# Soft-MoE after a gated recurrence: two weights moved behind the stream, and filler matmuls in TensorE's waits

## The chip, the cores and the metric

The kernel runs on one core of a Trainium2 chip. The core has five engines with queues of their own: TensorE (PE; its weight loads are shown apart as PEld), VectorE (DVE), ScalarE (ACT), GpSimd (POOL) and SyncE (SP). They share an on-chip memory (SBUF), TensorE writes into an accumulation memory (PSUM), and 16 DMA engines move data between HBM and SBUF. The metric is the device time of one execution in microseconds; lower is better. The version before takes 200.91 us (median of 13 runs, 199.79 to 202.6).

## The reference

Two layers, one after the other. The first is an elementwise gated recurrence over time for 4 sequences of 5056 tokens with 256 channels:

```
sig = 1/(1+exp(-f_logit));  f = lb + (1-lb)*sig;  i = 1 - f
for t: h = f[:,t]*h + i[:,t]*x[:,t];  y[:,t] = h
```

The second is a soft mixture of experts on the 4 x 5056 = 20224 rows of y: 8 experts with 4 slots each, 32 slots in all.

```
logits = y @ phi                        # [20224, 32]
d = softmax of logits over all rows;    slot_input = d.T @ y      # [32, 256]
slot_out[e] = relu(slot_input[e] @ w1[e]) @ w2[e]                 # w1: 256x1024, w2: 1024x256
c = softmax of logits over the slots;   out = c @ slot_out        # [20224, 256]
```

x and f_logit are 20.7 MB each, the eight pairs of expert weights 16.8 MB in f32, and the output 20.7 MB. All must be read or written once. No output row can be made before the experts are done, and they need the slot inputs, which need every row of y.

## The kernel before

**The stream.** Time is cut into 10 groups of 512 tokens (the ninth, `odd`, has 448), and each group has 4 units, one for each sequence: 40 units, numbered n = group * 4 + sequence. Inputs come in pairs of units, into three pair buffers of x and three of f (`ld`, bufs=3); SyncE issues them with `load(n + 6)` at every even n. A unit goes through these steps:

- `gate` (L199, ScalarE): s = sigmoid(-f), for two units at once from unit 6 on; an activation-table load stands around each change between sigmoid and exp.
- `enter` (L210, GpSimd): u = s * x.
- `s_to_channels`, `u_to_channels` (L225, TensorE): four 128x128 transposes each, so that channels lie on partitions; s for two units at every even n, u for one unit at every n.
- `decay` (L248, ScalarE): the factor a from s. `scan` (L258, VectorE): the recurrence, two instructions of 512 steps.
- `to_tokens` (L271, TensorE): four transposes of h back, into the single PSUM buffer `hp`; `keep_tokens` (L285) copies them into `ht`, on VectorE for even sequences and on ScalarE for odd ones. The next `to_tokens` needs that buffer empty.
- per group: `logits` (L299), `exps` (L308, into `etall`), `weights_to_tokens` (L320, L323) and `slots` (L349, which adds up 32 slots x 256 channels in PSUM, `slot_ps`).

The order of all this is written out by hand: the loop over n names, for each engine, what it does in that unit, and each engine runs its instructions in that order (the pools allow no reordering: `manual_schedule`). So in an even unit n TensorE does `to_tokens(n - 1)`, eight transposes of s for units n + 2 and n + 3, and four of u for unit n + 1, on which the next scan waits. An odd unit has no transposes of s. The units before and after a group's logits and slots have little TensorE work; the change calls for filler in some of them.

**The expert weights.** They are 16 transfers (w1 of experts 1 to 8, then w2 of experts 1 to 8), issued by GpSimd with a cast from f32 to bf16, each 1.05 MB read and 0.52 MB written. `W_AT` says in which unit how many are issued; the issue stands in GpSimd's queue after `enter(n + 3)`.

**The experts.** After the last unit, TensorE turns the slot sums into `sin`, and then: hidden layer of all experts (L551), transposes (L566), second layer of experts 1 to 4 packed into one pass (L587), then of experts 5 to 8 one after the other (L597, index j = 0 to 3, eight matmuls each). After j = 1 come the remaining row sums of the softmax over slots (L332, `row_sums`) into the PSUM tile `tail`. `spin` and `idle` are matmuls whose result nobody reads.

**The output.** `slot_out` (L610) is the last result that everything waits for; then TensorE multiplies (L630, L679), VectorE and ScalarE scale (L620, L624, L684, L690), and SyncE issues the stores.

The constant `rep` (four 32 x 128 copies of an identity, L87) is first used after the stream, at L522.

Of the kernel before, what the change touches and what calls it, by code (L numbers as in the profile page):

```python
# [10 lines left out]
BF16 = mybir.dt.bfloat16  # L11
# [7 lines left out]
def kernel(  # L19
# [10 lines left out]
    nc = tc.nc  # L30
    B, S, D = x.shape
    E = moe_w1.shape[0]
    F = moe_w1.shape[2]
    NS = moe_phi.shape[1]
    SPE = NS // E
    P = 128
# [5 lines left out]
    n_unit = n_grp * B  # L42
# [25 lines left out]
    ident_f = consts.tile([P, P], F32, name="ident_f")  # L68
# [12 lines left out]

    nc.vector.tensor_copy(ident, ident_f)

    def rep_constants():
        for b in range(B):
            blk = ident_f[ds(b * NS, NS), ds(b * NS, NS)]
            nc.vector.tensor_copy(rep[ds(b * NS, NS)],  # L87
                                  blk.unsqueeze(1).broadcast_to([NS, B, NS]))

    ones = consts.tile([P, B], BF16, name="ones")  # L90
    nc.vector.memset(ones, 0.0)
# [47 lines left out]
            nc.tensor.matmul(dst[:, ds(0, w)], w1_sb[0][:, 0, :P], w1_sb[0][:, 0, :w],  # L139
                             start=True, stop=True, skip_group_check=True)  # L140

    W_AT = {9: 1, 15: 1, 21: 1, 27: 1, 31: 1, 33: 1, 34: 3, 35: 1, 36: 6}
    w_next = [0]
    ctx.enter_context(tc.manual_schedule())

# [3 lines left out]
    with tc.tile_pool(name="sp2", bufs=3) as sp2, \  # L149
# [9 lines left out]
        slot_bank = pslot.tile([P, 2, D], F32, name="slot_ps")  # L159
        slot_ps = slot_bank[:, 0]  # L160

        def idle(k):
            for _ in range(k):
                nc.tensor.matmul(slot_bank[:, 1], w1_sb[0][:, 0, :P], w1_sb[0][:, 0, :D],
                                 start=False, stop=False, skip_group_check=True)
        xs, fs, sts, uts, pss, psus, hs, hps, hts, lgs, ets = ({} for _ in range(11))

        def tokens(src, n, k):
# [94 lines left out]
        SINGLE = 6  # L263
# [17 lines left out]
        def keep_tokens(n):  # L281
            g, b = divmod(n, B)
            n_p = rows(g)
            copy = nc.scalar.copy if b % 2 and n >= SINGLE - 2 else nc.vector.tensor_copy
            copy(hts[g][:n_p, b].rearrange("p r d -> p (r d)").bitcast(F32),  # L285
                 hps.pop(n)[:n_p].rearrange("p r c -> p (r c)"))

# [67 lines left out]
        def unit(f, m):  # L355
            if 0 <= m < n_unit:
                f(m)
# [63 lines left out]
        for n in range(n_unit):  # L421
            if n < SINGLE - 2:
                if n:
                    unit(to_tokens, n - 1)
                    unit(u_to_channels, n + 1)
                s_to_channels(n + 2)
                gate(n + 3, 1 if n + 3 < SINGLE else 2)
                decay(n + 2, 1)
                if n % 2 == 0:
                    unit(load, n + AHEAD)  # L430
                unit(enter, n + 3)
            else:
                end = n >= n_unit - 6
                if n % 2 == 0:
                    unit(load, n + AHEAD)
                    if n == SINGLE - 2:
                        to_tokens(n - 1)
                        keep_tokens(n - 1)
                    if not end:
                        unit(gate, n + 4)  # L440
                else:
                    unit(decay, n + 1)
                    if n == n_unit - 5:
                        gate(n + 3)
                        exps(odd - 1)
                if not end and n != n_unit - 7:
                    group(exps, n - 2)

                unit(enter, n + 3)
                for _ in range(W_AT.get(n, 0)):  # L450
                    load_w(w_next[0])
                    w_next[0] += 1

                if n == n_unit - 2:
                    unit(u_to_channels, n + 1)
                if n != SINGLE - 2:
                    unit(to_tokens, n - 1)
                if n == n_unit - 2:
                    keep_tokens(n - 1)
                if n % 2 == 0:  # L460
                    unit(s_to_channels, n + 2)
                    unit(s_to_channels, n + 3)
                if n != n_unit - 2:
                    unit(u_to_channels, n + 1)
                if n in (n_unit - 5, n_unit - 4):
                    idle(4)
                if n == n_unit - 2:
                    tail = psp.tile([P, 2, G], F32, name="tail", tag="sp")
                    rs_ps = tail[:, 0, ds(0, n_grp * R * B)].rearrange(
                        "p (q b) -> p q b", b=B)  # L470
                    late_ps, odd_ps = (
                        tail[:, 1].bitcast(BF16)[:, ds(i * R * P, R * P)].rearrange(
                            "p (r s) -> p r s", r=R) for i in range(2))
                    logits(odd)
                    exps(odd)
                    slots(odd - 1)
                    spin(tail[:, 1], 1, G)
                    odd_weights()
                elif not end:
                    group(logits, n - 1)  # L480
# [4 lines left out]
                late_weights([0, 1, 2], nc.scalar.copy)  # L485

            unit(scan, n)
            if n == 0:
                rep_constants()
            if n not in (SINGLE - 2, n_unit - 2):  # L490
                unit(keep_tokens, n - 1)
            if n == n_unit - 3:
# [32 lines left out]
    with tc.tile_pool(name="ew", bufs=1) as ew, \  # L525
# [69 lines left out]
        for j in range(Q):  # L595
# [8 lines left out]
            if j == 1:  # L604
                for i in range(1, len(blocks)):
                    row_sums(i)
                q = n_grp * R - 1
                nc.vector.reciprocal(rrow[:, wide_r:q], rs_ps[:, wide_r:q])
                nc.vector.reciprocal(rrow[:, q, ds(0, B // 2)], rs_ps[:, q, ds(0, B // 2)])
        nc.vector.tensor_scalar_mul(slot_out, so_ps, rcs)  # L610
# [141 lines left out]
```

## Time and profile before

| what | value |
|---|---|
| time, median of 13 runs | 200.91 us (199.79 to 202.6) |
| time of the profiled execution | 200.91 us |
| its span, first to last instruction | 199.1 us |
| TensorE busy / its weight loads | 133.5 us / 95.9 us |
| VectorE busy | 146.0 us |
| ScalarE busy | 137.8 us |
| GpSimd busy | 100.7 us |
| HBM read, written | 58.23 MB, 20.71 MB |
| mean granted TensorE clock | 0.839 |

The stream takes the first 130 us, the experts follow to 145.3, the output goes on to the end. A row by slices has 40 digits of 5 us each, in tenths of the slice; PEclk is the TensorE clock granted by the throttle, in tenths of full speed. A row by windows has the stretch and its length, then busy time and count of each engine (PE, PEld, DVE, ACT, POOL), the granted clock, the share of the DMA engines that was busy (it reads slightly over 1 when they are full) and the GB/s written. A timeline row has start, length, engine, line, operation, tiles and shapes, count, and in brackets how long the engine stood idle before it and what ended that. The chain of waits is followed back from the last instruction; its rows have start, length and what. L numbers are lines of the kernel before.

### The profile page before, as it was taken

What the parts mean: (1) busy time and instruction counts of PE and PEld (TensorE: products, weight loads), DVE (VectorE), ACT (ScalarE), POOL (GpSimd) and SP (SyncE); (2) the same over time, 40 slices, a digit from 0 to 9 for tenths busy, and PEclk for the clock granted to TensorE, in tenths of its full rate; (3) what the DMA queues carried; (4) which work ended last, traced back from release to release, by engine and by line L of the source; (5) the groups of instructions that cost most, each with busy time, mean ns of one, the idle gap of its engine ahead of it and who ended that gap; (6) DMA issues with size and microseconds to landing.
All of it is one profiled execution on the core that took longest, in us unless ns stands there. A gap on an engine that the chain in (4) does not pass through costs nothing.

```text
span 199.1 us, 3008 instructions
## 1 busy us (share of the span) xinstructions
PE 133.5 (67%) x1073; PEld 95.9 (48%) x1073; DVE 146.0 (73%) x168; ACT 137.8 (69%) x194; POOL 100.7 (51%) x72
## 2 busy tenths in 40 slices
PE   0585463975869667585976876999979999960000
PEld 0364352853657556464766555676853533410000
DVE  1699899699997999979999899915267877850000
ACT  2688666999988999599996498444057889990000
POOL 2388586894989379962995849950030000000000
PEclk9999999699996999979998899999995555555555
DMA  4999999999999999999999999999639999999995
GB/s 181 414 420 420 421 420 417 420 417 311 416 417 376 358 419 416 317 413 411 408 312 406 322 231 214 206 216 214 129 112 384 435 444 421 421 421 457 434 421 214
DMA packets 17614, 70.74 MB, mean 355 GB/s; under 512 B 2096, under 2 KB 3120, under 8 KB 16704
## 3 DMA queue, kind: packets, MB, share of 16 engines
q1 hardware_dynamic: 15120, 62.13, 76.2%
q0 software_dynamic: 2336, 8.42, 21.1%
q8 instruction: 8, 0.13, 0.2%
q14 instruction: 6, 0.05, 0.1%
q10 hardware_dynamic: 144, 0.00, 0.0%
HBM read 58.23 MB, written 20.71 MB: 396 GB/s over the span
## 4 chain that ended last, share of the span: by engine, by line
PE 35%; DVE 28%; DMA 15%; issue 8%; ACT 4%; SPq 1%; ACTq 0%; DVEq 0%
DVE h L258 21%; PE op L679 12%; DMA f_t<-in_f_logit_dram 10%; PE hp L271 4%; DMA x_t<-in_x_dram 4%; DVE ht L285 4%; PE sp L225 4%; PE op L630 2%; PE up L225 2%; PE so_ps L597 2%; ACT oc L690 1%; PE tail L332 1%; SPq L189 1%; PE hi_ps L551 1%; DVE et L323 1%
## 5 line engine op out<-in xcount | busy, mean ns | idle before, releaser
L210 POOL TENSOR_TENSOR u_t<-s_t,x_t 128x1024 bf16<-128x1024 bf16 (+1 forms) x39 | 82.4, 2128 | 28.2 <-ACT s_t L199 19.9
L258 DVE TENSOR_TENSOR_SCAN h<-a,h,up 128x512 bf16<-128x512 f32 (+1 forms) x72 | 86.3, 1250 | 5.4 <-PE up L225 3.8
L271 PE MATMUL hp<-ident_f,h 128*128 128x128 f32 (+1 forms) x160 | 30.8, 318 | 31.3 <-DVE ht L285 19.3
L199 ACT ACTIVATE s_t<-f_t 128x2048 bf16<-128x2048 f32 (+2 forms) x23 | 38.4, 1672 | 15.1 <-DMA f_t<-in_f_logit_dram 12.9
L248 ACT ACTIVATE a<-sp,nomlb 128x1024 f32<-128x1024 bf16 (+2 forms) x46 | 43.3, 994 | 3.0 <-PE sp L225 1.6
L271 PEld LDWEIGHTS hp<-ident_f,h 128*128 128x128 f32 (+1 forms) x160 | 22.9, 208 | 41.3 <-DVE ht L285 23.8
L225 PE MATMUL sp<-ident_f,s_t 128*128 128x128 f32 x144 | 23.7, 313 | 9.4 <-ACT s_t L199 6.1
L679 PE MATMUL op<-slot_bd,etall 64*128 64x512 bf16 x62 | 24.9, 622 | 0.3 <-ACT oc L690 0.2
L225 PEld LDWEIGHTS sp<-ident_f,s_t 128*128 128x128 f32 x144 | 19.8, 164 | 10.8 <-issue 6.0
L225 PE MATMUL up<-ident_f,u_t 128*128 128x128 f32 x144 | 24.3, 295 | 0.7 <-POOL u_t L210 0.7
L690 ACT ACTIVATE oc<-op,rrow 128x256 f32<-128x256 f32 x60 | 22.7, 488 | 2.1 <-PE op L679 1.5
L684 DVE TENSOR_TENSOR oc<-op,rrow 128x1024 f32<-128x1024 f32 x16 | 19.3, 1222 | 5.3 <-PE op L679 5.3
L225 PEld LDWEIGHTS up<-ident_f,u_t 128*128 128x128 f32 x144 | 18.9, 155 | 1.8 <-POOL u_t L210 1.1
L285 DVE COPY ht<-hp 128x512 f32<-128x512 f32 (+1 forms) x22 | 14.7, 669 | 2.1 <-PE hp L271 2.1
L679 PEld LDWEIGHTS <-etall 64*128 64x128 bf16 x62 | 9.1, 155 | 14.7 <-issue 12.6
L285 ACT COPY ht<-hp 128x512 f32<-128x512 f32 (+1 forms) x18 | 10.3, 575 | 4.7 <-PE hp L271 4.6
L624 ACT ACTIVATE ob<-op,rrow 128x256 f32<-128x256 f32 x16 | 6.3, 479 | 7.9 <-PE op L630 7.8
L258 DVE TENSOR_TENSOR_SCAN h<-a,up 128x512 bf16<-128x512 f32 x8 | 9.4, 1210 | 0.7 <-PE up L225 0.7
L612 POOL TENSOR_SCALAR slot_bd<-slot_out,parity 128x256 bf16<-128x256 bf16 x2 | 1.8, 920 | 13.4 <-DVE slot_out L610 13.4
L299 PE MATMUL lg<-h,phi 128*32 128x512 bf16 (+1 forms) x80 | 7.3, 414 | 0.0
L630 PE MATMUL op<-slot_out,etall 32*128 32x256 bf16 x32 | 5.9, 339 | 1.0 <-DVE slot_out L610 0.6
L349 PE MATMUL slot_ps<-ht,et 128*32 128x256 bf16 (+1 forms) x144 | 5.5, 274 | 0.8 <-DVE et L323 0.8
(98 smaller groups left out, 118.2 us busy)
## 6 DMA issues: line engine op xcount, KB each, us to landing
f_t<-in_f_logit_dram SPq DMA_DIRECT2D x36, 512.0 KB, 10.2
x_t<-in_x_dram SPq DMA_DIRECT2D x36, 512.0 KB, 10.5
out_dram<-oc SPq DMA_DIRECT2D x6, 2048.0 KB, 12.7
w_sb<-in_moe_w_dram POOLq DMA_DIRECT2D x16, 512.0 KB, 8.2
out_dram<-oc SPq DMA_DIRECT2D x4, 896.0 KB, 5.2
out_dram<-ob SPq DMA_DIRECT2D x1, 2048.0 KB, 8.3
f_t<-in_f_logit_dram SPq DMA_DIRECT2D x4, 384.0 KB, 7.7
x_t<-in_x_dram SPq DMA_DIRECT2D x4, 384.0 KB, 7.1
```

The costliest lines, as they stand in the source:

```text
L199: nc.scalar.activation(s_t, f_t, ACT.Sigmoid, scale=-1.0)
L210: nc.gpsimd.tensor_tensor(uts[n][:, :r], s_t[:, :r], x_t[:, :r], ALU.mult)
L225: nc.tensor.transpose(ps[:, :, r], t[:, r], ident_f)
L248: nc.scalar.activation(decays[n // 2, o][:, ds(n % 2, k), :T], sp[:, ds(n % 2, k), :T, o], ACT.Identity, scale=nomlb[:, ds(o, 1)], bias=1.0)
L258: nc.vector.tensor_tensor_scan(h[:, :T, o], decays[n // 2, o][:, n % 2, :T], up[:, :T, o], hs[n - B][:, ds(used(n // B - 1) - 1, 1), o] if ...
L271: nc.tensor.transpose(hp[:n_p, r], hw[:, :n_p, r], ident_f)
L285: copy(hts[g][:n_p, b].rearrange("p r d -> p (r d)").bitcast(F32), hps.pop(n)[:n_p].rearrange("p r c -> p (r c)"))
L299: nc.tensor.matmul(lg[ds(b * NS, NS), :], phi[:, o], hs[g * B + b][:, :T, o], start=o == 0, stop=o == DC - 1, skip_group_check=True)
L630: nc.tensor.matmul(op[:, j], ew[:, :, r + j], slot_out[ds(b * NS, NS)], start=True, stop=True, skip_group_check=True)
L679: nc.tensor.matmul(op[:, i_r].rearrange("p u d -> p (u d)"), ew[:, :, r + i_r], slot_bd[ds(j * 2 * NS, 2 * NS)].rearrange("s u d -> s (u d)"),
L684: nc.vector.tensor_tensor(ob[:, :, ds(r, k)].rearrange("p u r d -> p r u d"), op[:, ds(0, k)], scale[:, ds(r, k)].unsqueeze(3).broadcast_t ...
L690: nc.scalar.activation(ob[:, u, r + i_r], op[:, i_r, u], ACT.Copy, scale=scale[:, r + i_r, ds(u, 1)])
```

## The change

- `W_AT`: of the weights issued before unit 30, those at 9, 15, 21 and 27 become two, at 17 and 25. Six are issued at units 30 to 34 (before: five at units 31 to 34), none at 35, and eight instead of six at 36.
- Fillers: after the transposes of u, units 5 to 35 with n mod 8 in 1, 2, 5, 6, 7 (20 units) get five 256-column matmuls each. The operands of `idle` are now the identity and `rep` instead of the first weight, so that it waits for no weight.
- `rep` is therefore built at the start, by GpSimd, a quarter in each of units 0 to 3 behind `enter(n + 3)`, instead of by VectorE in unit 0.
- 28 matmuls of 32 columns (`SPINS`) go behind the row sums, between the second layers of experts six and seven (j = 1 and j = 2).
- `keep_tokens` changes engine for six units: 9, 17, 25 go from ScalarE to VectorE, and 12, 20, 28 from VectorE to ScalarE.
- In unit 3, ScalarE does `decay(5)` before the first paired gate instead of after it.

```diff
--- before.py
+++ after.py
@@ -81,11 +81,9 @@
 
     nc.vector.tensor_copy(ident, ident_f)
 
-    def rep_constants():
-        for b in range(B):
-            blk = ident_f[ds(b * NS, NS), ds(b * NS, NS)]
-            nc.vector.tensor_copy(rep[ds(b * NS, NS)],
-                                  blk.unsqueeze(1).broadcast_to([NS, B, NS]))
+    def rep_constants(b):
+        blk = ident_f[ds(b * NS, NS), ds(b * NS, NS)]
+        nc.gpsimd.tensor_copy(rep[ds(b * NS, NS)], blk.unsqueeze(1).broadcast_to([NS, B, NS]))
 
     ones = consts.tile([P, B], BF16, name="ones")
     nc.vector.memset(ones, 0.0)
@@ -139,7 +137,8 @@
             nc.tensor.matmul(dst[:, ds(0, w)], w1_sb[0][:, 0, :P], w1_sb[0][:, 0, :w],
                              start=True, stop=True, skip_group_check=True)
 
-    W_AT = {9: 1, 15: 1, 21: 1, 27: 1, 31: 1, 33: 1, 34: 3, 35: 1, 36: 6}
+    SPINS = 28
+    W_AT = {17: 1, 25: 1, 30: 1, 31: 1, 32: 1, 33: 2, 34: 1, 36: 8}
     w_next = [0]
     ctx.enter_context(tc.manual_schedule())
 
@@ -159,10 +158,12 @@
         slot_bank = pslot.tile([P, 2, D], F32, name="slot_ps")
         slot_ps = slot_bank[:, 0]
 
-        def idle(k):
-            for _ in range(k):
-                nc.tensor.matmul(slot_bank[:, 1], w1_sb[0][:, 0, :P], w1_sb[0][:, 0, :D],
-                                 start=False, stop=False, skip_group_check=True)
+        rep_bf = rep.rearrange("p b s -> p (b s)").bitcast(BF16)
+
+        def idle(k, first=False):
+            for i in range(k):
+                nc.tensor.matmul(slot_bank[:, 1], ident, rep_bf,
+                                 start=first and i == 0, stop=False, skip_group_check=True)
         xs, fs, sts, uts, pss, psus, hs, hps, hts, lgs, ets = ({} for _ in range(11))
 
         def tokens(src, n, k):
@@ -281,7 +282,10 @@
         def keep_tokens(n):
             g, b = divmod(n, B)
             n_p = rows(g)
-            copy = nc.scalar.copy if b % 2 and n >= SINGLE - 2 else nc.vector.tensor_copy
+            by_scalar = b % 2 and n >= SINGLE - 2
+            if 2 * B < n < n_unit - 2 * B and n % (2 * B) in (1, B):
+                by_scalar = not by_scalar
+            copy = nc.scalar.copy if by_scalar else nc.vector.tensor_copy
             copy(hts[g][:n_p, b].rearrange("p r d -> p (r d)").bitcast(F32),
                  hps.pop(n)[:n_p].rearrange("p r c -> p (r c)"))
 
@@ -424,11 +428,15 @@
                     unit(to_tokens, n - 1)
                     unit(u_to_channels, n + 1)
                 s_to_channels(n + 2)
-                gate(n + 3, 1 if n + 3 < SINGLE else 2)
+                if n + 3 < SINGLE:
+                    gate(n + 3, 1)
                 decay(n + 2, 1)
+                if n + 3 == SINGLE:
+                    gate(n + 3)
                 if n % 2 == 0:
                     unit(load, n + AHEAD)
                 unit(enter, n + 3)
+                rep_constants(n)
             else:
                 end = n >= n_unit - 6
                 if n % 2 == 0:
@@ -464,6 +472,8 @@
                     unit(u_to_channels, n + 1)
                 if n in (n_unit - 5, n_unit - 4):
                     idle(4)
+                elif SINGLE - 2 < n < n_unit - 4 and n % (2 * B) in (1, 2, 5, 6, 7):
+                    idle(5, n == SINGLE - 1)
                 if n == n_unit - 2:
                     tail = psp.tile([P, 2, G], F32, name="tail", tag="sp")
                     rs_ps = tail[:, 0, ds(0, n_grp * R * B)].rearrange(
@@ -485,8 +495,6 @@
                 late_weights([0, 1, 2], nc.scalar.copy)
 
             unit(scan, n)
-            if n == 0:
-                rep_constants()
             if n not in (SINGLE - 2, n_unit - 2):
                 unit(keep_tokens, n - 1)
             if n == n_unit - 3:
@@ -605,6 +613,7 @@
                 for i in range(1, len(blocks)):
                     row_sums(i)
                 q = n_grp * R - 1
+                spin(tail[:, 1], SPINS, NS)
                 nc.vector.reciprocal(rrow[:, wide_r:q], rs_ps[:, wide_r:q])
                 nc.vector.reciprocal(rrow[:, q, ds(0, B // 2)], rs_ps[:, q, ds(0, B // 2)])
         nc.vector.tensor_scalar_mul(slot_out, so_ps, rcs)
```

## The prediction

> **What bounds the kernel now.** I read first the page's rows by slices of the span, for what is never idle.
>
> ```profile
> PEclk9999999699996999979998899999995555555555
> DMA  4999999999999999999999999999639999999995
> HBM read 58.23 MB, written 20.71 MB: 396 GB/s over the span
> ```
>
> The DMA row is full from the second slice to the end but for one dip near 142 to 148 us. (GB/s counts bytes as written; a weight is read in f32, 1.05 MB, and lands in bf16, 0.52 MB. So 420 in the stream and about 212 while only weights move are the same reading speed.) Next the busy time by short windows around that dip:
>
> ```profile
> 120.00:140.00 20.00, 17.62 (x282) 12.84 (x281) 12.97 (x21) 10.38 (x22) 12.40 (x15) 1.00 1.06 212
> ...
> 142.00:143.00 1.00, 1.00 (x19) 1.00 (x18) 0.00 (x0) 0.00 (x0) 0.00 (x0) 1.00 0.47 94
> 143.00:144.00 1.00, 1.00 (x16) 0.94 (x16) 0.47 (x1) 0.00 (x0) 0.00 (x0) 1.00 0.05 8
> ...
> 146.00:147.00 1.00, 0.59 (x6) 0.47 (x5) 0.42 (x1) 0.47 (x1) 1.00 (x2) 1.00 0.00 0
> ```
>
> The reader should see that the last weight drains until about 144, that nothing moves for three microseconds, and that the output then fills the queues to the end. The view of the weight tiles says the last weight was issued at 126.5 and landed 17.6 us later: 144.1. The timeline of that stretch shows what TensorE does meanwhile:
>
> ```profile
> 141.13 1.04 PE L597 MATMUL so_ps<-w_sb,wide 128*128 128x256 bf16 x8
> 142.00 1.47 PE L332 MATMUL tail<-ones,etall 128*128 128x4 bf16 x23
> 143.35 1.91 PE L597 MATMUL so_ps<-w_sb,wide 128*128 128x256 bf16 x16
> 145.30 0.48 DVE L610 TENSOR_SCALAR slot_out<-so_ps,rcs 128x256 bf16<-128x256 f32 x1 [1.01 <-PE so_ps L597]
> 146.70 4.53 SPq L656 DMA_DIRECT2D out_dram<-ob  x8
> ```
>
> The 16 matmuls at 143.35 are experts seven and eight; one takes 0.27, so they start (1.91 - 0.27) / 15 = 0.109 us apart, so expert eight starts at 143.35 + 8 x 0.109 = 144.22. Its weight landed at 144.1. Two bounds end together: TensorE's chain reaches the last expert 0.1 us after the last weight is there. Whatever makes the chain shorter can win 0.1 us, and then the weight is waited for.
>
> Where does the chain come from? From VectorE's timeline and the chain of waits, in the stream:
>
> ```profile
> 60.04 2.44 DVE L258 TENSOR_TENSOR_SCAN h<-a,h,up 128x512 bf16<-128x512 f32 x2
> 63.76 2.45 DVE L258 TENSOR_TENSOR_SCAN h<-a,h,up 128x512 bf16<-128x512 f32 x2 [1.28 <-PE up L225]
> ...
> 83.50 2.44 DVE L258 TENSOR_TENSOR_SCAN h<-a,h,up 128x512 bf16<-128x512 f32 x2
> 87.27 2.45 DVE L258 TENSOR_TENSOR_SCAN h<-a,h,up 128x512 bf16<-128x512 f32 x2 [1.33 <-PE up L225]
> ```
>
> ```profile
> 60.17 1.13 PE hp L271 x4
> 61.30 1.71 PE sp L225 x8
> 63.01 0.72 PE up L225 x4
> ...
> 66.84 0.75 PE hp L271 x4
> 67.59 0.87 PE sp L225 x8
> 68.47 0.44 PE up L225 x4
> ```
>
> VectorE scans without a break except before units 9, 17, 25 and 33. There the same 16 transposes take 3.56 us instead of 2.06, because the granted clock is 0.50 from 60.02 to 63.44 (and at 36.1, 83.9, 107.8). Each time the window before had little TensorE work: 1.53 us of 3.41 from 56.61 to 60.02, 1.44 from 80.50 to 83.92.
>
> **The change part by part.** All is summed against the profiled execution: 200.91 us, span 199.1 and 1.8 around it. It is also the median of the 13 runs shown.
>
> *Fillers in light units.* 20 units get five 256-column matmuls: 5 x 0.109 = 0.55 us each, placed before TensorE's wait for the next copy (its transposes of line 271 stood idle 31.3 us over 40 units, so they hide there; with the cover gone each would delay a unit by 0.55). They raise the 1.4 to 1.5 us of the light windows to at least 2.0. In this trace windows of about that much busy time stayed warm (1.96 from 63.44 to 66.85), so I take the half clock as gone. Gain on VectorE's chain: 1.16 + 1.28 + 1.33 + 1.29 = 5.1 us, from nothing to that; I take 4 to 5, because ScalarE is busy 4.94 to 5.00 of each 5 us from 65 to 80 and may pace instead.
>
> In this trace the half-clock window from 60.02 to 63.44 holds transposes alone, all 16 of the chain lines above, and the clock is back at 1.00 after it: transposes count as work here. The Trainium skill, "TensorE: Matmul & The Clock Gate", part 4 (PE-mode transpose), says instead that transposes do not count as TensorE activity in the same way and leave the clock cold. By that rule 0.55 us of filler would be the window's only activity, no stretch would be saved, and the sum would be that of the second rival below; by the row it is that of the forecast.
>
> *Two weights fewer before unit 30.* A weight costs 0.524 MB / 212 GB/s = 2.47 us of transfer. Two fewer bring the inputs 4.9 us earlier, about what VectorE gains, so the feed keeps pace. Six at units 30 to 34 then compete with the last loads. The last x was issued at 104.1 and landed 14.1 later, at 118.2, behind six weights, the sixth not quite all. With five to seven in front it lands between 116 and 120; with a partial four, as sharing suggests, 114. Taken: 114, so the stream's end comes 4 us earlier, near 126.
>
> *The last weight.* No byte is added or removed. While the queues stay full, the sixteenth weight lands at 144.1 whatever the order: gain 0. The far end on the good side is a queue with no thin drain at all: the first 5 us moved 182 GB/s of 420, so transfers start in effect at 2.8, and 58.23 MB / 420 GB/s = 138.6 us more is 141.4, 2.7 us better; nothing in the change evens out the drain, so this is an end and not a case. At the other end they run dry. Stream and first eight weights are through at 144.1 - 8 x 2.47 = 124.3, and the other eight are queued on GpSimd behind enter(38), enter(39) and a gate of ScalarE. Without its unit 35 weight (0.6) GpSimd would have got there at 123.83 - 0.6 = 123.2, and the packets of a weight start 3.8 us after its issue (unit 9's: 41.6 to 45.4): 127.0. So the stream must gain 127.0 - 124.3 = 2.7 us or the queues stand empty for what is missing; before, with ten weights ahead, the same sum left 1.6 us to spare (129.2 against 127.6). With the 4 us above, 1.3 are spare. Taken: 0. The chain's 0.1 us is won.
>
> *28 fillers between experts six and seven.* The 22 small ones of line 139 take 0.70 us of weight loads, 0.032 each: 28 x 0.032 = 0.9 us. With weights landing at 139.2, 141.6 and 144.1 (2.47 apart), TensorE does expert six from 139.2 to 140.1, row sums (1.35) to 141.4, fillers to 142.3, expert seven to 143.2, and waits 0.9 us for the last. So they are hidden, by 0.9 us. If the chain were not earlier, all 0.9 would lie on it.
>
> *The rest.* Four copies into rep leave VectorE (3.33 us from 10.62 to 13.95, while DMA feeds the stream) and become four on GpSimd, after enter(3) to enter(6). Each costs between 0.27 (its 32x64 copy) and 0.82 (VectorE's mean); 0.5 taken, as a copy without arithmetic, nearer the first. GpSimd idles 0.3 to 0.4 us before each of these enters and 2.39 before the fourth, so 0. Three token copies go from VectorE (0.67) to ScalarE (0.57) and three come back: 0. At unit 3, decay goes ahead of a gate that waited 1.66 for its input: 0. Two more weight issues at unit 36 (0.56 each) delay GpSimd's memsets, which ended at 131.5 and are needed at 138.1: 0.
>
> Sum: 200.91 - 0.1 = **200.8 us**.
>
> **The rivals.**
> *A cold clock in the experts (slower).* TensorE now waits for each of the last four weights: 0.87 of matmuls in each 2.47, 35%, plus row sums and fillers. The windows that lost the clock in the stream had at most 1.74 of 3.41 busy (104.40 to 107.81). If the window before 144.1 falls among them, expert eight takes 8 x 0.109 more (0.9), and the first output matmuls (18 x 0.109 = 2.0 more, about a third of it ahead of their evictions) 0.7: 202.4. It decides once that window has under about 1.75 us busy. Against it: the fillers stand just there, and the window of the first 16 row sums, 128.29 to 131.70, shows 3.20 busy and stayed warm.
>
> *The stream gains too little (slower).* The fillers do not hold the clock, or ScalarE or late inputs pace the stream. Below a gain of 2.7 us the queues run dry before the last eight weights, and every microsecond missing comes on the last landing: with no gain it is 146.8, the 0.9 us of fillers are over by then, and the time is 200.9 + 2.7 = 203.6; with half the gain it is 202.2. Against it: the holes sit plainly behind the half clock, and the late inputs were ahead of their scans.
>
> *A better drain (faster).* The last drain is thin from 142 to 144 (DMA share 0.47, then 0.05: half a microsecond of work in two). If the DMA engines end together, 1.5 us of it goes: 199.4. For it: the runs reach 199.79. Against it: nothing in the change evens out engines.
>
> *The change does nothing that counts.* Then the time stays 200.9; it cannot be told from the forecast by time, only by the trace.
>
> **How the numbers follow.** About 0.5% (1.0 us) is what a measurement of this kernel tells from no change. Forecast, with the do-nothing case, 0.52, within 200.1 to 201.6. Cold clock 0.14. Too little gain 0.17. Better drain 0.17. Faster by over 0.5% (under 199.9) is the better drain: 0.17. Slower (over 201.9) is the cold clock and nearly all of too little gain: 0.30. Within: 0.53. The range takes in the better drain's end, half the missing gain and the cold clock: 199.4 to 202.5; outside are the empty queue at its worst and mishaps.
>
> **What would show it.** The clock row should be full from 10 to 125 us, with no 1.3 us holes before units 9, 17, 25 and 33; the last scan should end near 125 instead of 129. The DMA row should stay full to 142, and the last weight land at 144.0 to 144.3. Expert eight should begin within 0.1 us of that landing after an idle TensorE, 0.109 us apart if warm, 0.21 if cold. Wrong would be: a last landing over 0.8 us away from 144.1, a DMA gap between 15 and 142, or a first output issue not 2.6 us after that landing, as now.

## The result, and the profile after

The changed kernel takes 203.15 us (median of 11 runs, 201.17 to 204.77), the kernel before 200.88 (48 runs, 199.79 to 202.74): 1.0091 of the time, 95% interval 1.0058 to 1.0123. It is slower, and the forecast of 200.8 and its range of 199.4 to 202.5 miss it. Measured again on another occasion it took 202.81 us (12 runs, 200.97 to 205.22) against 201.22, a ratio of 1.0058 [1.0025, 1.0091]. Ratios and their intervals leave out executions that ran more than 1.5% above the shortest of the same kernel (two of these 11), so they are not the quotients of the medians.

The profiled execution is the shortest of those 11: 201.17 us, span 199.4. It must be read with that in mind. The rows by slices and the HBM line of the changed kernel's page:

```profile
PEclk9999999699999988999999999999685555555555
DMA  5999999999999999999999999999529999999994
HBM read 58.23 MB, written 20.71 MB: 396 GB/s over the span
```

They are what the forecast said: no hole in DMA until 142, and fewer half-clock windows. Next come the rows by windows (columns as before: stretch, length, five engines, clock, DMA share, GB/s):

```profile
120.00:122.00 2.00, 1.22 (x25) 0.84 (x23) 2.00 (x3) 0.60 (x1) 2.00 (x5) 1.00 1.10 211
122.00:125.00 3.00, 3.00 (x40) 2.14 (x38) 3.00 (x4) 1.51 (x4) 2.84 (x6) 1.00 1.02 201
140.00:145.00 5.00, 4.50 (x59) 3.44 (x57) 0.76 (x2) 0.00 (x0) 0.00 (x0) 0.66 0.50 100
```

and the timeline around the last weight:

```profile
141.35 1.87 PE L605 MATMUL so_ps<-w_sb,wide 128*128 128x256 bf16 x8
143.72 1.53 PE L605 MATMUL so_ps<-w_sb,wide 128*128 128x256 bf16 x8 [0.50 <-DMA w_sb<-in_moe_w_dram]
145.29 0.48 DVE L619 TENSOR_SCALAR slot_out<-so_ps,rcs 128x256 bf16<-128x256 f32 x1 [2.98 <-PE so_ps L605]
146.83 2.10 PE L639 MATMUL op<-slot_out,etall 32*128 32x256 bf16 x14 [0.63 <-DVE ob L629]
146.91 4.70 SPq L665 DMA_DIRECT2D out_dram<-ob  x8
```

The last weight lands at 143.7, TensorE waits 0.5 us for it, and expert seven runs at half clock (1.87 us for eight matmuls) in a window from 141.35 to 144.76. The last scan ends at 125.69, 3.23 us earlier than before. So this one execution does most of what was forecast, in its time too; but half-clock windows remain in the stream (from 35.54 and from 73.08 us). Of 26 executions of the changed kernel on record (the 11, one more that the median leaves out, the 12 and the two below), 5 are under 202 us and 21 over. The question is what the others do.

### The profile page after: what moved, and what is told of

It reads as the page before. It is cut to its first block, busy times and chain, and to the rows that moved or that the text cites. A ratio compares the mean times of both kernels' runs of the same rounds, so it can differ in the third digit from the quotient of the medians.

```text
span 199.4 us, 3263 instructions
## 1 busy us (share of the span) xinstructions
PE 142.7 (72%) x1201; PEld 103.1 (52%) x1201; DVE 142.8 (72%) x164; ACT 138.0 (69%) x194; POOL 101.5 (51%) x76
## 4 chain that ended last, share of the span: by engine, by line
PE 27%; DMA 25%; DVE 22%; issue 8%; POOL 4%; ACT 3%; SPq 1%; ACTq 0%; DVEq 0%; POOLq 0%
DVE h L259 18%; PE op L688 12%; DMA f_t<-in_f_logit_dram 10%; DMA w_sb<-in_moe_w_dram 10%; DMA x_t<-in_x_dram 4%; PE hp L272 3%; PE sp L226 3%; PE op L639 3%; DVE ht L289 3%; PE up L226 2%; POOL w_sb L132 2%; POOL u_t L211 2%; ACT oc L699 1%; PE slot_ps L165 1%; SPq L190 1%
## 5 line engine op out<-in xcount | busy, mean ns | idle before, releaser
L272 PE MATMUL hp<-ident_f,h 128*128 128x128 f32 (+1 forms) x160 | 29.6, 309 | 19.4 <-DVE ht L289 16.0
L272 PEld LDWEIGHTS hp<-ident_f,h 128*128 128x128 f32 (+1 forms) x160 | 22.8, 208 | 28.1 <-DVE ht L289 19.8
L226 PE MATMUL sp<-ident_f,s_t 128*128 128x128 f32 x144 | 21.7, 295 | 11.3 <-ACT s_t L200 7.5
L226 PEld LDWEIGHTS sp<-ident_f,s_t 128*128 128x128 f32 x144 | 17.7, 152 | 13.2 <-issue 5.7
L226 PEld LDWEIGHTS up<-ident_f,u_t 128*128 128x128 f32 x144 | 18.2, 152 | 2.2 <-POOL u_t L211 1.5
L165 PE MATMUL slot_ps<-rep,ident 128*128 128x256 bf16 x108 | 15.9, 279 | 0.0
L165 PEld LDWEIGHTS <-ident 128*128 128x128 bf16 x108 | 10.8, 100 | 1.2
```

Of the source, the lines that this page charges most:

```text
L165: nc.tensor.matmul(slot_bank[:, 1], ident, rep_bf, start=first and i == 0, stop=False, skip_group_check=True)
L226: nc.tensor.transpose(ps[:, :, r], t[:, r], ident_f)
L272: nc.tensor.transpose(hp[:n_p, r], hw[:, :n_p, r], ident_f)
```

## Experiments

### The changed kernel again, and two more profiles

No edit in any of the three: the changed kernel, once timed again and twice profiled alone.

> The changed kernel once more, unchanged, for a second profile. Theory 'dry queue': in most executions the stream ends later than in the first profile (125.7 us), so that the unit 36 weights are issued after 120.0 and their packets begin after 124: this profile shows a stretch of DMA below half its rate between 122 and 128 us and the last weight landing after 144.5; time 202.5 to 203.5. Theory 'cold experts': the queues stay full to 142, the last weight lands at 143.7 to 144.1, and the extra time lies between that landing and the first output store; the granted clock is 0.50 in two or more windows after 135 us; time also 202.5 to 203.5. Theory 'filler in the way': the stream ends later than 125.7 with the queues full, and the experts with it.

Measured: 202.81 us (200.97 to 205.22), ratio 1.0058 [1.0025, 1.0091]. Its profiled execution was again the shortest (200.97), with the last scan at 125.75 and the last weight at 144.0. The loss repeats, but no profile showed it yet.

> The changed kernel unaltered, for the profile of another execution. Theory (dry queue): in an execution above 202 us the eight weights of unit 36 are issued at 121.5 us or later, the DMA share falls short by 1 us or more between 120 and 130, and the last weight lands at 145 or later; in one below 201.5 they are issued near 120 and the last weight lands near 143.7. Rival (cold clock in the experts): the slow execution has its last weight at 143.6 to 144.3 and loses its time after that, in matmuls of expert eight 0.21 us apart.

> As the run before it, the same kernel once more: the same two readings, by the last weight's landing (145 or later with the queue dry, 143.6 to 144.3 with the cold experts).

Measured: 204.68 us and 203.96 us, two of the long executions. VectorE's timeline in the first of them (idle time ahead of an instruction stands in brackets):

```profile
53.74 7.14 DVE L259 TENSOR_TENSOR_SCAN h<-a,h,up 128x512 bf16<-128x512 f32 x6 [1.26 <-PE up L226]
77.17 7.14 DVE L259 TENSOR_TENSOR_SCAN h<-a,h,up 128x512 bf16<-128x512 f32 x6 [1.29 <-PE up L226]
100.22 2.45 DVE L259 TENSOR_TENSOR_SCAN h<-a,h,up 128x512 bf16<-128x512 f32 x2 [0.91 <-PE up L226]
```

The holes behind the half clock are back, 1.26 + 1.29 + 0.91 us of them, eight units apart as before, only ahead of other units (13, 21 and 29 in place of 17, 25 and 33; the one ahead of unit 9 is still there, 1.35 us, and in the short execution too, 1.13). The last scan ends at 128.86, in the other execution at 128.83, and before the change at 128.92: the stream gained nothing. What precedes each half-clock window, by TensorE's own busy time (window, length, busy and count, clock, DMA share, GB/s):

```profile
46.57:49.98 3.41, 1.51 (x24) 1.00 1.02 419
70.46:73.87 3.41, 1.31 (x23) 1.00 1.03 344
94.35:97.77 3.42, 1.32 (x23) 1.00 1.03 404
```

These lie on units 11, 19 and 27, three of the light units that got no filler (n mod 8 = 3). The windows that grant the clock are 3.41 us long, and eight units take 23.4 us with one half-clock window among them (units 16 to 24 here), close to seven windows (23.9): so a light window meets the windows at nearly the same place in every round. In the short execution, after the window ahead of unit 9, only one such window, 69.66 to 73.08 with 1.32 busy, cost the clock.

The end of the stream, in the same execution, by windows and in GpSimd's timeline:

```profile
120.00:122.00 2.00, 1.06 (x9) 0.75 (x8) 1.99 (x3) 1.99 (x5) 2.00 (x2) 1.00 1.07 213
122.00:125.00 3.00, 2.22 (x34) 1.84 (x34) 3.00 (x4) 1.76 (x2) 3.00 (x5) 1.00 0.77 142
140.00:145.00 5.00, 4.75 (x75) 4.24 (x74) 0.72 (x3) 0.00 (x0) 0.00 (x0) 1.00 1.02 205
```

```profile
118.98 4.25 POOL L211 TENSOR_TENSOR u_t<-s_t,x_t 128x1024 bf16<-128x1024 bf16 x2 [2.76 <-PE hp L272]
123.18 4.29 POOL L132 DMA_DIRECT2D w_sb<-in_moe_w_dram  x8
```

The eight weights of unit 36 are issued at 123.18, behind GpSimd's last two products; the eight ahead of them are through at 125.0, and the queue runs thin (0.77 of full from 122 to 125). The last weight lands at 146.6, and at 147.2 in the other execution; the first output store is issued 2.7 us after each. The rival of cold experts is out for both: expert eight's matmuls take 1.03 us there, the full clock.

### One part undone, one part alone

Before's weight order in the changed kernel, so that everything else of the change remains:

```diff
-    W_AT = {17: 1, 25: 1, 30: 1, 31: 1, 32: 1, 33: 2, 34: 1, 36: 8}
+    W_AT = {9: 1, 15: 1, 21: 1, 27: 1, 31: 1, 33: 1, 34: 3, 35: 1, 36: 6}
```

> The changed kernel with the weights issued in the units of the kernel before (ten before unit 36); fillers and all else stay. Dry queue: with ten weights ahead the queues hold until 129 us, so the loss goes: 200.5 to 201.3. Cold experts: TensorE waits for the last weights as before the edit, so the loss stays: 202.5 to 203.5. Filler in the way: stays, 202.5 to 203.5.

Measured: 201.26 us, ratio 1.0004 [0.9973, 1.0036], in the range of the dry queue. And the reverse, the kernel before with only the new weight order:

```diff
-    W_AT = {9: 1, 15: 1, 21: 1, 27: 1, 31: 1, 33: 1, 34: 3, 35: 1, 36: 6}
+    W_AT = {17: 1, 25: 1, 30: 1, 31: 1, 32: 1, 33: 2, 34: 1, 36: 8}
```

> The kernel before with only the units of the weight issues changed to those of the changed kernel; no filler, no other edit. Dry queue: the stream ends at 129 as before, the unit 36 weights are issued at 123.2 and begin at 127.0, the queues are empty from 124.3, and the last weight lands 2.7 us later: 203.4 to 203.9, with a dip to under 100 GB/s written between 124 and 128 us. Cold experts, without a dry queue: within 0.5 us of before.

Measured: 204.2 us, ratio 1.0143 [1.0089, 1.0197], 0.3 us over the range of the dry queue. So all of the loss comes with the weight order; the other edits together neither cost nor win measurably by themselves, and take back a third to three fifths of what the order costs. Two stretches of this kernel's windows show where the time goes:

```profile
100.00:105.00 5.00, 3.99 (x44) 3.12 (x43) 3.88 (x4) 3.71 (x4) 4.62 (x4) 0.92 0.93 335
120.00:125.00 5.00, 3.60 (x32) 3.12 (x32) 4.98 (x6) 4.91 (x7) 4.85 (x4) 1.00 0.83 167
125.00:130.00 5.00, 4.62 (x64) 3.04 (x64) 5.00 (x6) 1.74 (x4) 5.00 (x9) 1.00 0.88 159
```

The queues are thin at two places: at the end of the stream, and already at 100 us, in the middle of it.

### How many weights go ahead of unit 36

One weight fewer ahead of unit 36 (seven), and two more (ten, as before the change):

```diff
-    W_AT = {17: 1, 25: 1, 30: 1, 31: 1, 32: 1, 33: 2, 34: 1, 36: 8}
+    W_AT = {17: 1, 25: 1, 30: 1, 31: 1, 32: 1, 33: 2, 36: 9}     # seven
...
+    W_AT = {17: 1, 25: 1, 30: 1, 31: 1, 32: 1, 33: 2, 34: 3, 36: 6}     # ten
```

> The changed kernel with one weight more moved from unit 34 to unit 36: seven ahead, nine at unit 36. Dry queue: the queues are through one weight earlier, 2.47 us more stand empty: 204.8 to 205.6. Cold experts or filler in the way: no change, 202.5 to 203.2.

> The changed kernel with two of the eight weights of unit 36 issued at unit 34 instead (three there, six at 36); the two that left the stream's first 30 units stay out. Dry queue: 5 us more of work stand ahead of the unit 36 weights, so the loss goes: 200.5 to 201.3. Cold experts and filler in the way: 202.5 to 203.5.

Measured: 205.66 us with seven, 202.81 to 203.15 with eight, 201.04 with ten (ratio to before 0.9989 [0.9954, 1.0025]). The seven-weight kernel moved 104 of 420 GB/s from 120 to 125 us (bytes read, a weight counted in f32). Moving two weight issues from unit 36 to unit 34 takes back all of the loss, although the order up to unit 33 is the changed kernel's.

### Three weights issued one unit earlier

This keeps eight weights ahead of unit 35, and only lets three of the last eight be issued ahead of GpSimd's last product instead of behind it:

```diff
-    W_AT = {17: 1, 25: 1, 30: 1, 31: 1, 32: 1, 33: 2, 34: 1, 36: 8}
+    W_AT = {17: 1, 25: 1, 30: 1, 31: 1, 32: 1, 33: 2, 34: 1, 35: 3, 36: 5}
```

> The changed kernel with three of unit 36's eight weights issued at unit 35, ahead of GpSimd's last product and of what that waits for; the number ahead of unit 35 stays eight. Theory (the queue runs dry because the last eight issues wait on GpSimd behind the last two products): three weights are 7.4 us of transfer, the queue no longer empties, and the time comes back to 201.0 to 201.8 us against 202.8 to 203.2 for the changed kernel. Rival (it is the two weights that were taken from the front, and the later inputs, that cost): 202.5 to 203.2, as now.

Measured: 201.12 us (200.52 to 203.87), ratio 0.9983 [0.9949, 1.0017]: the theory's time. The profiled execution is a long one (202.47) and so a twin of the long execution shown above, with half-clock windows at the same places (49.98 and 50.02, 73.87 and 73.91, 97.77 and 97.80) and the last scan at 128.81. GpSimd's timeline of it, and its window:

```profile
118.93 2.14 POOL L211 TENSOR_TENSOR u_t<-s_t,x_t 128x1024 bf16<-128x1024 bf16 x1 [2.75 <-issue]
121.01 1.65 POOL L132 DMA_DIRECT2D w_sb<-in_moe_w_dram  x3
122.66 2.18 POOL L211 TENSOR_TENSOR u_t<-s_t,x_t 128x1024 bf16<-128x1024 bf16 x1
124.76 2.71 POOL L132 DMA_DIRECT2D w_sb<-in_moe_w_dram  x5
```

```profile
122.00:125.00 3.00, 2.10 (x33) 1.66 (x33) 3.00 (x4) 1.71 (x2) 3.00 (x4) 1.00 1.03 191
```

The same stream, no dry queue (1.03 against 0.77), and the last weight at 145.3 instead of 146.6 and 147.2. It is still 1.3 later than before's 144.0. Where that is from follows from the bytes. I counted the bytes read in each 5 us against 419 GB/s and so got the time by which the transfers fall behind, to about 0.1 us:

| profiled execution | lost from 80 to 115 us | lost from 120 to 130 us | last weight lands |
|---|---|---|---|
| before | 0.4 | 0 | 144.0 |
| changed, short | 0.4 | 0 | 143.7 |
| changed, long (204.68) | 1.9 | 1.0 | 146.6 |
| changed, long (203.96) | 1.8 | 1.5 | 147.2 |
| three weights at unit 35 | 1.3 | 0.25 | 145.3 |
| ten ahead of unit 36 (long) | 1.6 | 0 | 145.1 |

Subtracting before's 0.4, the two columns give the last column to within 0.4 us. So a long execution loses twice: once at the end, where the last eight weights come too late, and once in mid-stream. The execution in the last row (203.10 us) lost time in the experts as well: a half-clock window lies there, from 132.03 to 135.44, and its first store is issued 3.9 us after the last landing instead of 2.7. The second loss is the same two weights: they were 4.9 us of transfer ahead of unit 30, and when the stream does not run 4.9 us faster, the inputs run into their buffers. SyncE's queue of the long execution, over the whole span (who waited for whom, us in total, times, longest):

```profile
SPq L190 <- POOL u_t L211: 23.2, 11, 3.5
SPq L190 <- DMA f_t<-in_f_logit_dram: 15.3, 16, 1.6
```

The loads wait 23.2 us for GpSimd to free an x buffer, in the kernel before 9.5 us; for the f transfers 15.3 us, before 27.8. With before's weight order in the changed kernel the first is 9.9 us; in the short execution it is 19.8, without the mid-stream loss. So these waits go with the new weight order, and cost time only where the stream does not gain.

### Fillers in the units that had none

Five fillers also in units 11, 19 and 27, and 13 instead of 28 between experts six and seven, so that the number of matmuls stays:

```diff
-    SPINS = 28
+    SPINS = 13
...
-                elif SINGLE - 2 < n < n_unit - 4 and n % (2 * B) in (1, 2, 5, 6, 7):
+                elif SINGLE - 2 < n < n_unit - 4 and n % (2 * B) in (1, 2, 3, 5, 6, 7):
```

> The changed kernel with five fillers in units 11, 19 and 27 too, and 13 instead of 28 between experts six and seven, which keeps the number of instructions. Dry queue through the clock: the stretch of those units is where the clock still falls (1.3 us busy of 3.4 ahead of each half-clock window at 50, 73 and 98 us), so the windows go, the stream ends by 125.7 in nearly all executions and the queues hold: 200.8 to 201.8. If the clock is not what moves the stream's end: 202.5 to 203.2.

Measured: 203.76 us (202.63 to 205.39), ratio 1.0147 [1.0101, 1.0194]. It missed 200.8 to 201.8 and lies over the rival's range too. In its profiled execution (205.39 us, the longest of the six) the stream did become faster: no half-clock window from 27 to 115 us, eight units in 22.0 us, and the scan of unit 36 began at 113.0, where it was 118.0 in the long execution and 114.8 in the short one. But then GpSimd waits:

```profile
117.25 2.13 POOL L211 TENSOR_TENSOR u_t<-s_t,x_t 128x1024 bf16<-128x1024 bf16 x1 [5.97 <-DMA x_t<-in_x_dram]
121.04 2.14 POOL L211 TENSOR_TENSOR u_t<-s_t,x_t 128x1024 bf16<-128x1024 bf16 x1 [1.66 <-DMA x_t<-in_x_dram]
123.12 4.30 POOL L132 DMA_DIRECT2D w_sb<-in_moe_w_dram  x8
```

The last x, issued at 99.3, lands 21.5 us later, at 120.9, because the weights of units 30 to 34 are issued earlier too and share the queues with it. The last eight weights stand behind that x in GpSimd's order, at 123.1 again, and the transfers lose 2.6 us between 120 and 130. (From 146.07 on the clock is at half as well, and the first store is issued 3.6 us after the last landing instead of 2.7.) A faster stream alone does not help: the time of the last eight issues is set by the slower of the stream and the last x. With the two weights moved to unit 34, or three to unit 35:

```diff
-    W_AT = {17: 1, 25: 1, 30: 1, 31: 1, 32: 1, 33: 2, 34: 1, 36: 8}
+    W_AT = {17: 1, 25: 1, 30: 1, 31: 1, 32: 1, 33: 2, 34: 3, 36: 6}     # ten ahead of 36
...
+    W_AT = {17: 1, 25: 1, 30: 1, 31: 1, 32: 1, 33: 2, 34: 1, 35: 3, 36: 5}     # three at 35
```

> The same fillers, and two weights of unit 36 at unit 34. Dry queue: nothing is left but the bytes; the last weight lands at 143.5 to 144.1 in nearly all executions: 200.3 to 200.9, with a smaller spread than before. If the fillers are in the way: 201.0 to 202.0.

> The kernel with fillers also in units 11, 19 and 27 (203.76 us), with the same move of three weights from unit 36 to unit 35. Its stream waits for the last x, which lands at 120.8 us behind the weights, and the last eight weights are issued only after that, at 123.1. Theory: with three issued ahead of the last wait for x the queue stays full, 201.0 to 201.8 us. Rival (the late x itself costs, through the stream's end): 203 to 204, as now.

Measured: 201.46 us (ratio 1.0016 [0.9984, 1.0048]) and 200.8 us (200.16 to 202.09, ratio 0.9988 [0.9953, 1.0023]). The first missed 200.3 to 200.9, although its last weight landed at 143.8 as that theory said: in its profile the clock falls to half at 146.75, the first 14 output matmuls take 2.87 us, and the output lasts 0.8 us longer than before's (52.0 against 51.2, from the first store's issue to the last landing). The time lies in the range of "fillers in the way", which was not tested apart from that. The second has everything that the forecast wanted, the last scan at 125.35 and the last weight at 143.8 in its profiled execution, and it equals the kernel before: the bytes end at 144 either way. It is the best of the kernels tried, and not measurably better than before.

### The fillers themselves

None between experts six and seven, with eight weights ahead and with ten:

```diff
-    SPINS = 28
+    SPINS = 0
```

> The changed kernel without the 28 fillers between experts six and seven. Dry queue: the fillers run while a weight is on its way, so nothing changes: 202.5 to 203.5. Cold experts: fewer busy microseconds ahead of the last experts, so more of them run at half clock: 203 to 204.5. If instead the fillers themselves are late on the path, 0.9 us less: 202 to 202.4.

> Two of the weights of unit 36 issued at unit 34, as in the earlier run with that edit, and no filler between experts six and seven. Dry queue alone: no change against that run, 200.8 to 201.4, since the fillers stand where a weight is awaited. If the fillers keep the clock up for the last experts: 201.9 to 202.9, with half the clock in a window that holds expert seven or eight. If they cost time: 200.2 to 200.6.

Measured: 204.71 us against 202.81 of the changed kernel, and 202.52 against 201.04. The kernels without these fillers, which were costed at nothing, are 1.9 and 1.5 us slower. The first lies over every range of its expectation. The second is in the range of "the fillers keep the clock up", but its profile has no half-clock window from 100.44 to 148.23, so none on expert seven or eight. In that profile the last weight lands at 143.8 and the first store is issued at 146.53, before's being 144.0 and 146.70, and yet the last store lands at 198.8, 0.9 later than before. The view of the DMA queues from 151 to 157.5 us in it (queue: packets, MB, share of 16 engines):

```profile
q1 hardware_dynamic: 653, 2.53, 95.5%
q8 instruction: 1, 0.02, 0.9%
```

One 16 KB packet of TensorE's instructions, from 151.57 to 152.53, occupies one DMA engine for 0.96 us among the stores; the store issued at 149.04 took 5.25 us to land where its counterpart before took 3.33. That such packets are TensorE's is read from their number: 8 in the profiles with 2146 matmuls and weight loads, 9 with 2346 and 2402, 10 with 2602, one in about 256. Before and after the change the last one falls at 145.0 and 144.7, into the gap between weights and output: the change adds 128 matmuls with 128 weight loads, exactly one packet. To tell this from the clock, the 28 small matmuls were put into unit 6, with the number kept; and the kernel before got 100 small matmuls in units 5, 6, 7, 9 and 10, to shift the packets:

```diff
+                if n == 6:     # with SPINS = 0, ten weights ahead of unit 36
+                    for _ in range(28):
+                        nc.tensor.matmul(slot_bank[:, 1, ds(0, NS)], ident, ident[:, ds(0, NS)],
...
+                if n in (5, 6, 7, 9, 10):     # in the kernel before
+                    for _ in range(20):
+                        nc.tensor.matmul(slot_bank[:, 1, ds(0, NS)], ident, ident[:, ds(0, NS)],
```

> Two weights of unit 36 at unit 34, no filler between experts six and seven, but 28 matmuls of 32 columns in unit 6 instead, so that TensorE has as many instructions as the changed kernel. Theory 'fetch': without the 28 fillers TensorE's instruction fetch (16 KB, one of every 256 instructions) falls into the output instead of the gap before it, and holds one DMA engine for 0.95 us there; with the count restored the last fetch lies near 145 again: 200.8 to 201.5. Theory 'clock': the fillers keep the last experts at full clock, so taking them from there costs as before: 202.2 to 202.9.

> The kernel before with 100 matmuls of 32 columns (200 instructions with their weight loads) spread over units 5, 6, 7, 9 and 10, where TensorE waits; nothing else. Fetch: the count is 56 short of a whole block more, so the last fetch moves from 145 to about 151 us, into the output: 201.9 to 202.5, and the profile shows a 16 KB instruction packet after 150 us. Without an effect of the fetch: 200.9 to 201.5.

Measured: 201.83 us, between the two theories, and 202.4 us (ratio 1.009 [1.0053, 1.0127]), in the range of the fetch; the packet is at 152.19 in the latter and back at 144.60 in the former. But not all of the latter's loss is the packet's. Its profiled execution is 1.5 us longer than before's; 0.8 of that is the output (52.0 us from the first store's issue to the last landing, instead of 51.2), and 0.7 lies ahead of it: the last scan ends at 129.66 instead of 128.92, and the first store is issued at 147.41 instead of 146.70. Of the 1.5 us that the fillers' absence cost, about 0.7 (202.52 to 201.83) go with the packet and 0.8 (201.83 to 201.04) with the place of the fillers; each of the two is hardly more than the measurements tell apart (0.35% either way). The timeline of the kernel with the moved fillers shows what can cost the second part:

```profile
143.66 1.86 PE L609 MATMUL so_ps<-w_sb,wide 128*128 128x256 bf16 x8 [1.20 <-DMA w_sb<-in_moe_w_dram]
147.10 3.14 PE L643 MATMUL op<-slot_out,etall 32*128 32x256 bf16 x14 [0.43 <-DVE ob L633]
```

A half-clock window begins at 143.2: expert eight takes 1.86 us instead of 1.03, and the first output matmuls 3.14 instead of 1.90. This is the forecast's rival of the cold clock, in one execution. That the fillers' place keeps it away isn't shown: the short execution of the changed kernel had such a window with all 28 fillers in place, and the profile above with none of them had none. Last, twice as many fillers in the light units:

```diff
-                    idle(5, n == SINGLE - 1)
+                    idle(10, n == SINGLE - 1)
```

> The changed kernel with ten fillers in each of the 20 light units instead of five. If the stream's end varies with the half clock (dry queue through clock windows that five fillers do not always prevent): fewer half-clock windows between 40 and 120 us, an earlier and steadier stream, 201.0 to 202.0. If fillers are in TensorE's way: later than with five, 203.5 to 205.

Measured: 206.16 us, ratio 1.019 [1.0119, 1.0262], over both ranges. Its profile has a half-clock window at 74.0, and the last scan at 129.23; the transfers lose 2.3 us from 80 to 115 and 1.5 from 120 to 130, and an instruction packet lies in the output, at 156.4. Ten fillers are 1.1 us of TensorE per unit and may no longer hide in full; I did not separate these.

## Why the prediction was wrong, point by point

*"I take the half clock as gone. Gain on VectorE's chain: ... I take 4 to 5."* This is the step that failed. The gain is 3.2 us in the two short executions profiled and 0.1 us in the two long ones. Even the short ones keep half-clock windows ahead of unit 9 and from 73.1, so 4 to 5 was too much for them too. It was read off one execution: the light windows found there were the ones that the fillers covered. Where the 3.41 us windows fall against the units differs from execution to execution (the scan of unit 8 starts at 36.4 to 36.5 in all four, the half-clock window near it at 35.54 and 35.61 in the short ones, at 36.33 and 36.49 in the long ones), and with another fall the light window lies on units 11, 19 and 27, which have no filler. Nor does busy time alone tell which window keeps the clock: in the profile before, 1.74 us of 3.41 was followed by the full clock (46.37 to 49.78) and by the half (104.40 to 107.81). Whether an execution is a long one because of that fall alone isn't shown: it is so in the four profiles of this kernel.

*"Two fewer bring the inputs 4.9 us earlier, about what VectorE gains, so the feed keeps pace."* Wrong with the first step. Without the gain the queues starve in mid-stream for 1.3 to 1.9 us, a loss that the prediction didn't have in any of its cases. The kernel with the weight order alone shows it too.

*"Taken: 114"* for the last x. It landed at 116.9 in the short execution and, with a faster stream, at 120.8: the six weights are issued by the same stream, so they come earlier with it and share the queues for longer.

*"So the stream must gain 127.0 - 124.3 = 2.7 us or the queues stand empty ... With the 4 us above, 1.3 are spare."* The condition was right and the spare was not there. With 3.2 us of gain the queue held, by 0.5 us on that sum; with 0.1 it ran dry. The rival drawn from this step, "the stream gains too little", said 146.8 for the last landing and 203.6 us with no gain; the runs gave 146.6 and 147.2, and a median of 203.15. It had a chance of 0.17. The agreement is partly luck: the end of the stream lost 1.0 and 1.5 us of the 2.6 and 3.1, and mid-stream the rest. The prediction counted 3.8 us from issue to packets. The Trainium skill, "DMA: Bandwidth & Descriptors" (Anatomy of one DMA), gives a fixed cost of some 2 us, most of it at completion. In the long execution shown, the traffic is low from 123.5 to about 125.2 and full again 2 to 2.5 us after the issue at 123.18, and in the kernel of 203.76 us 2.5 after its issue; the measured start is nearer the page's size than 3.8, although not at the completion end.

*"The last weight ... whatever order: gain 0"* and the chain's 0.1: right. In no execution profiled did the last weight land before 143.6, and the best kernel ends at before's time.

*"28 fillers ... hidden, by 0.9 us."* Right that they cost nothing: in the four profiles of the changed kernel TensorE still waits 0.5 to 1.4 us for the last weight behind them. That the kernels without them would be 1.5 to 1.9 us slower was not seen.

*The rest at nothing*: as a sum with the fillers, yes (1.0004 [0.9973, 1.0036] with before's weight order); not taken apart.

*The cold clock in the experts* came in the short execution (141.35 to 144.76), and cost about 0.5 us: 3.2 from last landing to first store instead of 2.7. The condition that the prediction set for it, under about 1.75 us busy in the window before, is wrong: that window, 137.94 to 141.35, had 3.03. And the window of the first 16 row sums, which it took as safe with 3.20 busy, lost the clock with 3.20 in three executions (the long one of 203.96, ten ahead, and seven ahead; half clock from 132.03 to 132.14 on). It isn't what makes the last weight late in the long executions.

*Transposes and the clock.* The kernel with three weights at unit 35 and fillers in every light unit has this window, which stayed warm, and this in it (TensorE's windows, then its timeline):

```profile
70.14:73.55 3.41, 1.86 (x28) 1.00 1.03 392
```

```profile
70.02 0.62 PE L353 MATMUL slot_ps<-ht,et 128*32 128x256 bf16 x16
72.18 0.75 PE L272 MATMUL hp<-ident_f,h 128*128 128x128 f32 x4 [1.55 <-DVE ht L289]
72.77 1.04 PE L226 MATMUL sp<-ident_f,s_t 128*128 128x128 f32 x8
```

Only 0.5 us of it is matmuls other than transposes, and in the short execution of the changed kernel the window from 93.56 to 96.98 holds 16 transposes alone (1.79 us busy) and kept the clock too. So transposes count here, as the prediction took it; not always enough, since from 18.94 to 22.35 the kernel shown here lost the clock with 1.93 us of transposes alone. The Trainium skill, "TensorE: Matmul & The Clock Gate", part 4 (PE-mode transpose), says otherwise; the measurement decides.

## What to carry to other kernels

A term that rests on a margin of 1.3 us must be priced over what varies between executions, not in the one that was profiled: here the end of the stream lay 3 us apart in executions whose clock windows fell differently, and the profile of the changed kernel happened to be its shortest run. When transfers are moved behind a stream, ask what the issuing engine stands behind at that moment: eight weights behind GpSimd's last two products were enough to run the queue dry, and issuing three of them one unit earlier took it all back in the median. Where bytes set the end, as here, a faster stream wins nothing, and a queue that runs empty loses.

## What the runs showed that was not expected

- TensorE's instructions are loaded by the same 16 DMA engines, 16 KB about once in 256 instructions, 0.9 to 1.0 us on one engine. A hundred idle matmuls near unit 7 of the kernel before moved such a load from 145 to 152 us, and the output then lasted 0.8 us longer in the profile; the kernel became 1.3 us slower, with the rest of it ahead of the output. Adding exactly 128 matmuls kept the load in the gap.
- How long the output lasts, from the first store's issue to the last landing, goes with where the clock falls to half: 51.0 to 51.3 us where the first 14 output matmuls take 1.9 to 2.2 us, 52.0 where they take 2.9, and 52.3 where they take 3.1, with no instruction packet among the stores in any (3.1 in the long execution of 204.68, the moved fillers, and the kernel of 203.76). So the execution of 204.68 us is 0.7 us longer than that of 203.96, although its first store is issued 0.55 us earlier.
